# Taking batch elements one at a time through two decode layers, with transposed keys kept and softmax for two heads at once

## Chip, cores and metric

The kernel runs on one core of one Trainium2 chip. The metric is device time in microseconds (us) of one execution; lower is better.

Engine names in the profile: PE is TensorE (matmul), PEld its weight loads, DVE VectorE, ACT ScalarE, POOL GpSimd, SP the engine that issues the transfers. The kernel keeps its tiles in two on-chip memories: SBUF, into which it loads data, and PSUM, into which it has TensorE write.

## The reference, cut to what matters

Two layers of grouped-query attention and a feed-forward network (FFN), for four batch elements of one new token each. Both layers use the same weights and the same key and value cache.

```python
# B = 4, D = 512, 32 query heads, 8 key/value heads, Sk = 4096, Dh = 128, F = 1792, bf16
q = (x @ wq) ...                                     # 4 query heads share one key head
scores = einsum("bhqd,bhkd->bhqk", q, k) * Dh**-0.5
o = einsum("bhqk,bhkd->bhqd", softmax(scores), v)
attn = o @ wo
x = x + attn(layernorm(x));  x = x + ffn(layernorm(x))     # layer 1
x = x + attn(layernorm(x));  x = x + ffn(layernorm(x))     # layer 2, same caches
```

Keys of one head are 1 MB, values as much: 32 element-head pairs of each, 67 MB, plus 13.9 MB of weights. A kernel that reads the caches anew in each layer moves 148 MB.

## The kernel before

It works layer by layer. In a layer, all 32 pairs of element and head go through a key stage (transpose the keys on TensorE, copy them out of PSUM, multiply with the queries, find the maximum), then all 32 through a value stage. The scheduler orders instructions, so the stages overlap somewhat.

```python
for j in range(NPAIR):                                # key stage, one head of one element
    K_j = issue_k(j)                                  # 1 MB, 8 KB per partition
    for g in range(NG):                               # 4 x 8 transposes
        for t in range(TB):
            nc.tensor.transpose(tp[:, t, :], K_j[:, g * TB + t, :], ident_bf[:, :])
        evac_copy(KT_j[:, g * TB:(g + 1) * TB, :], tp[:, :, :])     # DVE, DVE, ACT, DVE
    for c in range(C):
        nc.tensor.matmul(sc[:, c, :], lhsT=KT_j[:, c, :], rhs=qcols, start=True, stop=True)
    nc.scalar.activation(out=SCORES[:, j, :, :], in_=sc[:, :, :], func=ACT.Copy)
    nc.vector.tensor_reduce(out=colmax[:, :], in_=sc..., op=ALU.max)    # 3 buffers
    nc.gpsimd.partition_all_reduce(gmax[:, :], colmax[:, :], P, RED.max)
    nc.gpsimd.tensor_scalar(out=NEGB[:, j, :], in0=gmax[:, :], scalar1=-scale, ...)

for j in range(NPAIR):                                # value stage
    V_j = ...                                         # 1 MB
    for h in range(rep):                              # 4 small exponentials
        nc.scalar.activation(out=pexp[:, :, h], in_=SCORES[:, j, :, h], func=ACT.Exp,
                             bias=NEGB[:, j, h:h + 1], scale=scale, accum_out=SUMS[:, j, h:h + 1])
    nc.gpsimd.partition_all_reduce(den[:, :], SUMS[:, j, :], P, RED.add)
    nc.vector.reciprocal(out=rden[:, :], in_=den[:, :])
    for c in range(C):
        nc.tensor.matmul(ot[:, :], lhsT=V_j[:, c, :], rhs=pexp[:, c, :], ...)
    nc.vector.tensor_tensor(out=OT_bf[:, b, qsl], in0=ot[:, :], in1=rden[:, :], op=ALU.mult)
    # [cut: projection, FFN, next queries after every second element]
```

## Time and profile before

| | before |
|---|---|
| median of the first three runs | 599.63 us (596.45 to 600.38) |
| transfers | 149.22 MB, 250 GB/s on the mean |
| transpositions on TensorE | 2,048 |

These are lines of the page of the profile of before: busy time by engine, two rows of the 40 slices (the granted TensorE clock in tenths, and the busy share of the transfer engines in tenths), and the transfer queue of the data.

```profile
PE 321.7 (54%) x7448; PEld 310.1 (52%) x7448; DVE 189.1 (32%) x548; ACT 170.0 (28%) x644; POOL 66.2 (11%) x198
PEclk9976965886575555555556696777657765555555
DMA  8996992855957562565997493655433978545770
q1 hardware_dynamic: 26480, 148.13, 65.5%
```

No engine is near full, and GpSimd is the least busy. The next fence is the timeline of GpSimd in a key stage; the columns are start, duration, instructions, and in brackets the idle time before them and what ended it ("issue" means that nothing the profile shows was waited for).

```profile
386.40 1.10 POOL L263 PARTITION_ALL_REDUCE gmax<-colmax  x3 [8.56 <-issue]
394.94 0.86 POOL L264 TENSOR_SCALAR NEGB<-gmax 128x4 f32<-128x4 f32 x3 [7.45 <-DVE KT_j L218]
403.60 1.10 POOL L263 PARTITION_ALL_REDUCE gmax<-colmax  x3 [7.80 <-issue]
```

Three all-reduces, a gap, three tensor_scalars, a gap: 17.2 us (403.60 - 386.40) for three heads, 2 us of it busy. Within a row of three of one kind there is no gap. The second gap is put down to a VectorE copy, but is as long as the others.

TensorE, in the same stretch, stands for 7 us in each period:

```profile
404.37 1.84 PE L256 MATMUL sc<-qT_bf,KT_j 128*128 128x4 bf16 x64 [6.87 <-DVE colmax L260]
413.59 1.05 PE L251 MATMUL tp<-ident_bf,K_j 128*128 128x128 bf16 x16 [0.22 <-ACT KT_j L220]
421.59 1.84 PE L256 MATMUL sc<-qT_bf,KT_j 128*128 128x4 bf16 x64 [6.95 <-DVE colmax L260]
```

The table of waits sums such gaps (total us, times, longest us):

```profile
POOL gmax L263 <- issue: 135.6, 16, 11.4
DVE colmax L260 <- POOL gmax L263: 117.2, 19, 10.1
POOL NEGB L264 <- issue: 116.5, 14, 12.6
POOL NEGB L264 <- DVE KT_j L218: 66.9, 9, 10.0
POOL den L281 <- issue: 58.0, 7, 11.5
```

### The profile page before, as it was taken

The numbers are of one execution on the slowest core, as the hardware profiler recorded it, in microseconds if no ns is written. First come the engines' busy times: TensorE is split into PE (matmuls) and PEld (weight loads), VectorE is DVE, ScalarE is ACT, GpSimd is POOL, SyncE is SP. The second block draws the span as 40 slices with busy tenths as digits, with TensorE's granted clock in tenths as the row PEclk, the third lists the DMA queues.
The fourth block names the chain that finished last, engine by engine and source line by source line (L and its number), as shares of the span: only waits on it lengthen the run. The fifth ranks groups of instructions, "written<-read, shape, count | busy, mean of one in ns | idle before, by whom it ended". The sixth has DMA issues, their size and how long they took to land. (4 is left out here: it accounts for less than half of the span.)

```text
span 596.7 us, 17105 instructions
## 1 busy us (share of the span) xinstructions
PE 321.7 (54%) x7448; PEld 310.1 (52%) x7448; DVE 189.1 (32%) x548; ACT 170.0 (28%) x644; POOL 66.2 (11%) x198
## 2 busy tenths in 40 slices
PE   0998833757533410267578984466655573101555
PEld 0988733656533410267568984456655473101554
DVE  2554622534322100034135672344433331000213
ACT  0243511322112420233601344122211463112710
POOL 0001111101010111020200012101110111200300
PEclk9976965886575555555556696777657765555555
DMA  8996992855957562565997493655433978545770
GB/s 334 415 373 228 354 366 88 314 213 181 390 225 282 220 242 104 212 254 206 390 420 289 161 348 133 212 212 209 157 137 142 357 295 347 215 194 212 276 292 2
DMA packets 26555, 149.22 MB, mean 250 GB/s; under 512 B 2152, under 2 KB 8048, under 8 KB 10096
## 3 DMA queue, kind: packets, MB, share of 16 engines
q1 hardware_dynamic: 26480, 148.13, 65.5%
q8 instruction: 58, 0.95, 0.6%
q14 instruction: 17, 0.14, 0.1%
HBM read 148.12 MB, written 0.00 MB: 248 GB/s over the span
## 5 line engine op out<-in xcount | busy, mean ns | idle before, releaser
L251 PE MATMUL tp<-ident_bf,K_j 128*128 128x128 bf16 x2048 | 170.8, 254 | 7.6 <-ACT KT_j L220 6.0
L251 PEld LDWEIGHTS <-K_j 128*128 128x128 bf16 x2048 | 155.6, 117 | 12.7 <-issue 11.0
L218 DVE COPY KT_j<-tp 128x1024 bf16<-128x1024 bf16 x192 | 129.6, 689 | 66.0 <-PE tp L251 55.8
L256 PE MATMUL sc<-qT_bf,KT_j 128*128 128x4 bf16 x2048 | 63.6, 166 | 124.0 <-DVE colmax L260 123.2
L256 PEld LDWEIGHTS <-KT_j 128*128 128x128 bf16 x2048 | 63.2, 104 | 126.4 <-issue 125.2
L286 PE MATMUL ot<-pexp,V_j 128*128 128x4 bf16 x2048 | 61.2, 166 | 107.2 <-DVE OT_bf L288 92.0
L286 PEld LDWEIGHTS <-V_j 128*128 128x128 bf16 x2048 | 59.0, 104 | 109.0 <-issue 92.5
L277 ACT ACTIVATE pexp<-SCORES,NEGB 128x32 bf16<-128x32 f32 x256 | 86.3, 355 | 102.9 <-PE ot L286 101.6
L220 ACT ACTIVATE KT_j<-tp 128x1024 bf16<-128x1024 bf16 x64 | 65.4, 1021 | 110.2 <-PE tp L251 108.0
L258 ACT ACTIVATE SCORES<-sc 128x128 f32<-128x128 f32 x64 | 17.8, 279 | 180.6 <-PE sc L256 180.6
L260 DVE TENSOR_REDUCE colmax<-sc 128x4 f32<-128x128 f32 x64 | 18.5, 289 | 125.1 <-POOL gmax L263 117.2
L283 DVE RECIPROCAL rden<-den 128x4 f32<-128x4 f32 x64 | 11.2, 177 | 127.9 <-POOL den L281 126.9
L277 ACT ACTIVATION_READ_ACCUMULATOR pexp<-SCORES,NEGB 128x1 f32 x256 | 48.1, 188 | 0.0
L263 POOL PARTITION_ALL_REDUCE gmax<-colmax x64 | 23.9, 428 | 199.2 <-issue 135.6
L281 POOL PARTITION_ALL_REDUCE den<-SUMS x64 | 28.1, 469 | 103.3 <-issue 58.0
L264 POOL TENSOR_SCALAR NEGB<-gmax 128x4 f32<-128x4 f32 x64 | 15.0, 234 | 194.3 <-issue 116.5
L288 DVE TENSOR_TENSOR OT_bf<-ot,rden 128x4 bf16<-128x4 f32 x64 | 9.8, 156 | 43.4 <-PE ot L286 43.0
L172 PEld LDWEIGHTS <-wo_sb 128*128 128x128 bf16 x384 | 13.0, 103 | 7.5 <-issue 7.4
L172 PE MATMUL yT<-OT_bf,wo_sb 128*128 128x2 bf16 (+1 forms) x384 | 12.9, 166 | 6.4 <-DVE OT_bf L288 6.4
L162 PEld LDWEIGHTS <-wq_sb 128*128 128x128 bf16 x384 | 11.1, 103 | 7.9 <-issue 7.9
L162 PE MATMUL qps<-xnT_bf,wq_sb 128*128 128x2 bf16 (+1 forms) x384 | 11.1, 165 | 7.5 <-DVE xnT_bf L151 7.4
L183 PE MATMUL hg<-xnT_bf,wg_sb 128*128 128x2 bf16 (+1 forms) x168 | 4.9, 165 | 7.0 <-DVE xnT_bf L151 7.0
(82 smaller groups left out, 69.5 us busy)
## 6 DMA issues: line engine op xcount, KB each, us to landing
K_j<-in_A_k_cache_dram SPq DMA_DIRECT2D x64, 1024.0 KB, 6.3
V_j<-in_A_v_cache_dram SPq DMA_DIRECT2D x64, 1024.0 KB, 9.1
wq_sb<-in_A_wq_dram SPq DMA_DIRECT2D x2, 2048.0 KB, 13.2
wo_sb<-in_A_wo_dram SPq DMA_DIRECT2D x1, 4096.0 KB, 17.9
wg_sb<-in_B_w_gate_dram SPq DMA_DIRECT2D x1, 1792.0 KB, 10.8
wu_sb<-in_B_w_up_dram SPq DMA_DIRECT2D x1, 1792.0 KB, 14.9
wd_sb<-in_B_w_down_dram SPq DMA_DIRECT2D x1, 1792.0 KB, 19.4
x_bf<-in_A_x_dram SPq DMA_DIRECT2D x1, 4.0 KB
```

Source lines behind the costliest of these rows:

```text
L162: nc.tensor.matmul(qps[:, h, :], lhsT=wq_sb[:, k, m * Dh:(m + 1) * Dh], rhs=xnT_bf[:, k, bs], start=(k == 0), stop=(k == KD - 1))
L172: nc.tensor.matmul(yT[:, dk, :], lhsT=wo_sb[:, i, dk * P:(dk + 1) * P], rhs=OT_bf[:, bs, i], start=(i == 0), stop=(i == Hq - 1))
L218: nc.vector.tensor_copy(out=out_ap, in_=in_ap)
L220: nc.scalar.activation(out=out_ap, in_=in_ap, func=ACT.Copy)
L251: nc.tensor.transpose(tp[:, t, :], K_j[:, c, :], ident_bf[:, :])
L256: nc.tensor.matmul(sc[:, c, :], lhsT=KT_j[:, c, :], rhs=qcols, start=True, stop=True)
L258: nc.scalar.activation(out=SCORES[:, j, :, :], in_=sc[:, :, :], func=ACT.Copy)
L260: nc.vector.tensor_reduce(out=colmax[:, :], in_=sc.rearrange("p c h -> p h c"), axis=AX.X, op=ALU.max)
L263: nc.gpsimd.partition_all_reduce(gmax[:, :], colmax[:, :], P, RED.max)
L277: nc.scalar.activation(out=pexp[:, :, h], in_=SCORES[:, j, :, h], func=ACT.Exp, bias=NEGB[:, j, h:h + 1], scale=scale, accum_out=SUMS[:, j ...
L281: nc.gpsimd.partition_all_reduce(den[:, :], SUMS[:, j, :], P, RED.add)
L286: nc.tensor.matmul(ot[:, :], lhsT=V_j[:, c, :], rhs=pexp[:, c, :], start=(c == 0), stop=(c == C - 1))
```

## The change

Its intent is to read and transpose the keys once instead of twice. An element's transposed keys for its eight heads stay in SBUF, so the element must finish layer 1 and compute its layer-2 scores before the next element's keys replace them. Around that, softmax is rebuilt for pairs of heads: the maximum is subtracted on VectorE, so `NEGB` on GpSimd is gone. Tiles of K and V are halved to 0.5 MB, in seven buffers; the layer-2 values of an element are multiplied while the next element is between its layers. The diff is shortened.

```diff
-            nc.gpsimd.partition_all_reduce(gmax[:, :], colmax[:, :], P, RED.max)
-            nc.gpsimd.tensor_scalar(out=NEGB[:, j, :], in0=gmax[:, :], scalar1=-scale, ...)
-            for h in range(rep):
-                nc.scalar.activation(out=pexp[:, :, h], in_=SCORES[:, j, :, h], func=ACT.Exp,
-                                     bias=NEGB[:, j, h:h + 1], scale=scale, accum_out=SUMS[...])
+    def softmax(sc, pool):                             # for GH = 2 heads
+        nc.vector.tensor_reduce(out=colmax[:], in_=sc..., op=ALU.max)
+        nc.gpsimd.partition_all_reduce(gmax, colmax, P, RED.max)
+        nc.vector.tensor_tensor(out=sh[:], in0=sc[:], in1=gmax... , op=ALU.subtract)
+        nc.scalar.activation(out=pe[:], in_=sh[:], func=ACT.Exp, scale=scale)
+        nc.vector.tensor_reduce(out=ssum[:], in_=pe..., op=ALU.add)
+        nc.gpsimd.partition_all_reduce(den, ssum, P, RED.add)
+        nc.vector.reciprocal(out=rden[:], in_=den[:])
-    attention_layer(True, after_batch_l1)
-    attention_layer(False, after_batch_l2)
+    for b in range(B):
+        for g in range(NGRP):                          # 4 pairs of heads
+            for s in range(GH): keys(b, g * GH + s)    # load, transpose, keep in KT
+            prob1[g] = softmax(scores(b, g, q1_bf), p1p)
+            if g > 0: values(b, ...) of pair g - 1
+        values(b, ...) of the last pair
+        out_proj_add(b, 1, OT_bf); ffn(b, 1); layer_norm(b, 1); q_proj(b, 1, q2_bf, 2)
+        if prob2_prev is not None: values(b - 1, ...) of all heads, layer 2
+        prob2_prev = [softmax(scores(b, g, q2_bf), p2p) for g in range(NGRP)]
     # [cut: layer norm with fewer instructions, layouts, loads of the weights]
```

## The prediction

> **What bounds the kernel now.** Not bandwidth, not TensorE. The page gives TensorE 54%, VectorE 32%, ScalarE 28%, GpSimd 11% of 596.7 us; DMA moved 149 MB at 250 GB/s, while its best 15 us stretches reached 416 to 421 GB/s.
>
> GpSimd's timeline explains the rest. In the key stage (380 to 450 us) it repeats: three `gmax` all-reduces (1.10 us together), 7.5 us idle, three `NEGB` tensor_scalars (0.86 us), 7.8 to 8.4 us idle. One period of 17.2 us serves three heads. TensorE works about 9 us of it, then stands 7 us until `colmax`, which waits for `gmax`, has freed the score buffer. So GpSimd, "11% busy", sets the pace. The Trainium skill's "GPSIMD Engine Reference", section 2.1, says that the first call to a freshly loaded kernel pays about 6 us of code load with no visible instruction. This trace agrees in kind but shows 7 to 8.5 us, at each change between all-reduce and tensor_scalar. The table of waits sums the unexplained "issue" idle before `gmax`, `NEGB` and `den` to 310 us, plus 67 us before `NEGB` put down to a VectorE copy long ended. The instruction order has 49 such changes: 49 x 7.8 = 380 us.
>
> **What the change does.**
> - GpSimd: `NEGB` is gone and two heads share a reduce: 64 all-reduces (about 0.45 us each), one code load. This is the main gain: the 17.2 us period falls away.
> - Keys are loaded and transposed once: traffic 149 to about 115 MB; 1,024 transposes (about 65 us of TensorE) and 128 PSUM copies (65 us VectorE, 33 us ScalarE) go, mostly hidden.
> - 256 exponentials with accumulator reads (86 + 48 us) become 32, estimate 0.5 us each; VectorE gains 32 subtractions and 32 sums, estimate 0.3 to 0.45 us each.
> - Added: projections, FFN and norms run four times for one element instead of twice for two: 29 ns a matmul whatever the width, about 25 us of TensorE, and two more serial chains.
> - Packets halve from 8 to 4 KB; 4 KB ones take 159 ns here, 8 KB ones 309: little loss.
>
> **New bound: DMA, then the serial chain.** Loads: 24,576 packets of 159 to 176 ns over 16 engines, 244 to 270 us, plus about 40 us of weights: 285 to 310 us if never starved. TensorE needs about 250 us, more at a low clock, nearly a tie. Between layers DMA starves: out-projection, FFN, two norms, query projection and four softmaxes make a chain of 26 to 30 us (from the last chain before: norm 4.1, FFN 6, 29 ns a projection matmul), and seven half-megabyte buffers cover about 20 us of it. I count 7 us lost in each of four, 15 us from the last V to the end (17 before), 4 at the start, 10 to 20 for evacuation waits and low clock.
>
> 295 + 28 + 19 + 10 = **352 us**, range **322 to 400** (8 in 10). Faster by over 2%: 0.97; within: 0.02; slower: 0.01.
>
> **What would show it.** No "issue" gaps of 7 to 8 us on GpSimd, no wait of `colmax` on `gmax` over about 1 us; DMA share above 80% in first-layer stages, dips to half between layers; a chain of waits of DMA and the per-element chain. If my GpSimd reading is wrong, gaps remain without tensor_scalars.
>
> **What would make it wrong.** A low clock makes transposes (128 columns) near 107 ns, so TensorE overtakes DMA; or the in-order DMA queue blocks on a buffer whose reader waits in the chain: 380 us and more. If chains hide, 320 us.

## The result

The changed kernel takes 378.66 us (median of four runs, 375.91 to 379.92), against 598.95 us. The ratio is 0.6314, with a 95% interval of 0.6282 to 0.6346. Ratios here are the mean time of one kernel's fast runs over that of the other's fast runs of the same rounds, so not quite the ratio of the medians.

The same lines of the page after the change:

```profile
PE 275.4 (73%) x7268; PEld 263.8 (70%) x7268; DVE 137.5 (36%) x476; ACT 67.7 (18%) x90; POOL 25.0 (7%) x70
PEclk9999685555558667555596685555778855555555
DMA  7998999999258999947899999758999998579920
q1 hardware_dynamic: 35696, 114.58, 83.0%
```

Transfers are busy for 83.0% of the span, 313 us (0.83 x 377.3), and dip between the elements (the 2 and 5, the 4, and the two later 5s inside the DMA row). On GpSimd the gaps have gone. Its timeline in the first-layer stage of the third element shows one all-reduce at a time, waiting for VectorE:

```profile
211.25 0.36 POOL L236 PARTITION_ALL_REDUCE gmax<-colmax  x1 [9.88 <-DVE colmax L233]
213.20 0.40 POOL L248 PARTITION_ALL_REDUCE den<-ssum  x1 [1.59 <-DVE ssum L245]
222.48 0.37 POOL L236 PARTITION_ALL_REDUCE gmax<-colmax  x1 [8.88 <-DVE colmax L233]
```

The table of waits now shows these (the last two are those of the transfer queue, for a free buffer):

```profile
DVE sh L239 <- POOL gmax L236: 10.8, 23, 0.6
PE yT L159 <- DVE OT_bf L264: 16.4, 34, 1.2
SPq L104 <- PE ot L262: 100.6, 74, 5.7
SPq L104 <- PE tp L218: 97.8, 59, 11.1
```

VectorE's longest wait for `gmax` is 0.6 us, where before it was 10.1. The table of windows shows the two kinds of stage. A line gives start and end of a stretch and its length, then the busy time and number of instructions of PE, PEld, DVE, ACT and POOL, then the granted clock (1.00 is full speed), the share of the transfer engines, and GB/s.

```profile
100.00:110.00 10.00, 10.00 (x252) 10.00 (x250) 6.24 (x16) 3.07 (x5) 2.45 (x7) 0.50 0.31 82
160.00:170.00 10.00, 7.41 (x259) 7.27 (x257) 3.01 (x19) 0.00 (x0) 0.00 (x0) 0.50 0.44 125
170.00:180.00 10.00, 7.91 (x285) 7.68 (x283) 4.37 (x14) 1.25 (x3) 2.06 (x6) 0.50 0.65 210
200.00:210.00 10.00, 9.50 (x196) 9.35 (x196) 3.42 (x7) 4.19 (x5) 0.40 (x1) 0.66 1.01 388
```

The first three lie between layers and move 82 to 210 GB/s; the last lies in the first-layer stage and moves 388.

### The profile page after: what moved, and what is told of

The parts are those of the page before. It is cut to its first block, busy times and chain, and to the rows that moved or that the text cites. A ratio compares the mean times of both kernels' runs of the same rounds, so it can differ in the third digit from the quotient of the medians.

```text
span 377.3 us, 15723 instructions
## 1 busy us (share of the span) xinstructions
PE 275.4 (73%) x7268; PEld 263.8 (70%) x7268; DVE 137.5 (36%) x476; ACT 67.7 (18%) x90; POOL 25.0 (7%) x70
## 4 chain that ended last, share of the span: by engine, by line
PE 53%; DMA 16%; DVE 15%; issue 9%; ACT 3%; POOL 3%; SPq 1%; POOLq 0%; ACTq 0%; DVEq 0%
PE tp L218 19%; PE sc L227 14%; DMA v_t<-in_A_v_cache_dram 9%; PE ot L262 7%; DMA wd_sb<-in_B_w_down_dram 6%; PE qps L148 4%; DVE kt L207 2%; PE yT L159 2%; PE hg L170 2%; DVE colmax L233 2%; DMA k_t<-in_A_k_cache_dram 2%; DVE ssum L245 2%; ACT kt L205 2%; ACT pe L243 1%; PE st L114 1%
## 5 line engine op out<-in xcount | busy, mean ns | idle before, releaser
L218 PE MATMUL tp<-ident_bf,k_t 128*128 128x128 bf16 x1024 | 97.2, 271 | 1.2 <-DMA k_t<-in_A_k_cache_dram 0.6
L218 PEld LDWEIGHTS <-k_t 128*128 128x128 bf16 x1024 | 85.2, 125 | 2.0 <-issue 1.0
L262 PE MATMUL ot<-pe,v_t 128*128 128x4 bf16 x2048 | 69.0, 166 | 17.0 <-DMA v_t<-in_A_v_cache_dram 9.7
L262 PEld LDWEIGHTS <-v_t 128*128 128x128 bf16 x2048 | 63.0, 102 | 19.1 <-DMA v_t<-in_A_v_cache_dram 11.0
L227 PE MATMUL sc<-q_bf,kt 128*128 128x4 bf16 x2048 | 69.3, 166 | 9.1 <-DVE kt L207 3.1
L227 PEld LDWEIGHTS <-kt 128*128 128x128 bf16 x2048 | 64.4, 102 | 12.8 <-DVE kt L207 5.3
L205 ACT COPY kt<-tp 128x1024 bf16<-128x1024 bf16 x52 | 52.6, 1012 | 111.0 <-PE tp L218 93.9
L207 DVE COPY kt<-tp 128x1024 bf16<-128x1024 bf16 x76 | 51.7, 687 | 53.2 <-PE tp L218 51.6
L159 PE MATMUL yT<-OT_bf,wo_sb 128*128 128x1 bf16 (+1 forms) x640 | 22.2, 165 | 25.5 <-DVE OT_bf L264 16.4
L148 PE MATMUL qps<-xn_bf,wq_sb 128*128 128x1 bf16 (+1 forms) x640 | 18.4, 165 | 8.2 <-DVE xn_bf L136 6.6
```

What stands on the lines that cost most here:

```text
L148: nc.tensor.matmul(qps[:, i, :], lhsT=wq_sb[:, k, m * Dh:(m + 1) * Dh], rhs=xn_bf[:, bs, k], start=(k == 0), stop=(k == KD - 1))
L159: nc.tensor.matmul(yT[:, :, dk], lhsT=wo_sb[:, i, dk * P:(dk + 1) * P], rhs=o_bf[:, bs, i], start=(i == 0 and dk == 0), stop=(i == Hq - 1 ...
L205: nc.scalar.copy(out=out_ap, in_=in_ap)
L207: nc.vector.tensor_copy(out=out_ap, in_=in_ap)
L218: nc.tensor.transpose(tp[:, i, :], kn[:, g * TB + i, :], ident_bf[:, :])
L227: nc.tensor.matmul(sc[:, s, c, :], lhsT=KT[kvh][:, c, :], rhs=q_bf[:, b, kvh * rep:(kvh + 1) * rep], start=True, stop=True)
```

## The experiments

Twelve runs were made, each beside the kernel before on the same chip; one of them is the changed kernel once more. "Code load" stands for the unexplained gap at a change between the two kinds of GpSimd instruction: the name is taken from the prediction, and no trace shows a load itself. Theory A: before the change, GpSimd's code loads set the pace, and after it transfers and TensorE nearly tie, with transfers starving between the layers. Rival B: what counted was the second load and transposition of the keys. Rival C: the many small exponentials. Rival D: after the change TensorE alone is the limit.

### Code loads alone, taken out of the kernel before

```diff
-            nc.gpsimd.tensor_scalar(out=NEGB[:, j, :], in0=gmax[:, :], scalar1=-scale,
+            nc.vector.tensor_scalar(out=NEGB[:, j, :], in0=gmax[:, :], scalar1=-scale,
```

> The kernel before with one word changed: NEGB is computed on VectorE, so GpSimd runs nothing but all-reduces and loads code once instead of 49 times. Traffic (149 MB), 2,048 transposes and the 256 small exponentials all stay. Theory A (code loads set the pace before): 400 to 480 us, because the 17.2 us period of three heads in the key stage falls to TensorE's own 9 to 13 us. Rival B (the second load and transposition of the keys, that is bytes and TensorE work, is what the change saved): 570 us or more, since none of it is taken away. Rival C (the 256 exponentials on ScalarE): also 570 or more.

Measured: 421.51 us against 601.24, ratio 0.7016 (0.6985 to 0.7047). Of the whole gain (1 - 0.6314 = 0.3686) one word is worth 0.2984, that is 81%. It moves as many bytes and transposes as much as before, so B and C are not what made the kernel before slow; what they save once the gaps are gone, less what the rest of the change costs, is the other 19%. The page of this run:

```profile
PE 306.0 (73%) x7448; PEld 288.5 (69%) x7448; DVE 191.8 (46%) x612; ACT 175.4 (42%) x644; POOL 51.8 (12%) x134
PEclk9977999899995555555556669999999955555555
DMA  7999999999999999987998449999999999999900
q1 hardware_dynamic: 26480, 148.13, 89.8%
L251 PE MATMUL tp<-ident_bf,K_j 128*128 128x128 bf16 x2048 | 146.6, 231 | 1.5 <-DMA K_j<-in_A_k_cache_dram 1.0
```

The DMA row is nearly full from start to end: with the gaps on GpSimd gone, transfers bound this version. Its GpSimd timeline has a head every 3.1 us:

```profile
67.33 0.37 POOL L263 PARTITION_ALL_REDUCE gmax<-colmax  x1 [2.71 <-DVE colmax L260]
70.41 0.37 POOL L263 PARTITION_ALL_REDUCE gmax<-colmax  x1 [2.71 <-DVE colmax L260]
```

Before it was 17.2 us for three, 5.7 us a head.

### Code loads put back into the changed kernel

```diff
+        gm2 = grp.tile([P, GH, rep], FP32, name="gm2", tag="gm2", bufs=2)
+        nc.gpsimd.tensor_scalar(out=gm2[:], in0=gmax[:], scalar1=1.0, scalar2=None, op0=ALU.mult)
         sh = shp.tile([P, GH, C, rep], FP32, name="sh", tag="sh")
-                                in1=gmax[:].unsqueeze(2).broadcast_to([P, GH, C, rep]),
+                                in1=gm2[:].unsqueeze(2).broadcast_to([P, GH, C, rep]),
```

> The changed kernel with one GpSimd tensor_scalar (times 1.0, same values) put between each all-reduce maximum and its subtraction: 32 tiny operations, 44 more code loads in the instruction order. Theory A: about 7.8 us for most of those loads, 44 x 7.8 = 340 us of GpSimd time, largely on the path: 550 us or more, GpSimd gaps of 7 to 8 us back. Rival B: 32 operations of 0.25 us, under 390 us.

Measured: 496.27 us (one run, so its state is unknown), 118 us slower than 378.66. 32 operations of under 0.3 us each did that, so rival B is out here as well; but the time is under the 550 that was expected. The waits of GpSimd in this run:

```profile
POOL gm L239 <- issue: 185.6, 22, 12.5
POOL den L250 <- issue: 73.3, 12, 7.0
POOL gmax L236 <- issue: 16.5, 2, 10.1
```

The gaps are there, 275 us in these three lines, 8.4 us in the mean before `gm` (185.6 / 22), the result of the added operation. Only 118 us reached the end of the span. The size of a gap was right; "largely on the path" was not: other work went on during more than half of it. The kernel before is alike: its gaps sum to 377 us (the four GpSimd lines shown above), and taking them away gained 180. What the gaps are worth depends on what stands beside them: taken out of the kernel before, they are 81% of the gain; put back into the changed kernel, a smaller sum of them (275 us against 377) is 53% (118 of 220 us).

### Keys loaded and transposed again

```diff
-        prob2_prev = [softmax(scores(b, g, q2_bf), p2p) for g in range(NGRP)]
+        prob2_prev = []
+        for g in range(NGRP):
+            for s in range(GH):
+                keys(b, g * GH + s)
+            prob2_prev.append(softmax(scores(b, g, q2_bf), p2p))
```

> The changed kernel, but each element's keys are loaded and transposed again ahead of its second attention, as in the kernel before (traffic back to 149 MB, 2,048 transposes), with GpSimd as in the changed kernel. Tells what keeping the keys is worth once the code loads are gone. Theory A with a DMA bound: 34 MB more at 370 GB/s is 91 us, so 450 to 480 us, if the reload can't fill the DMA gaps between the layers; 420 to 440 if it fills them. Rival B: 550 or more.

Measured: 455.26 us, ratio 0.7591 (0.7549 to 0.7632). Keeping the keys is worth 77 us in this structure (0.7591 - 0.6314, times 600), against 91 us for the bytes at the mean rate. So it is not hidden. But this run moves the same bytes as the kernel before with `NEGB` on VectorE, has GpSimd as free, and is 34 us slower than it (455.26 against 421.51). That is what all the rest of the change costs on balance: going element by element, with smaller tiles, more and narrower projections, and softmax in pairs. No run separates these. It leaves the change 43 us ahead of the one-word edit.

Where do the 34 us go? The transfer queue of this run:

```profile
q1 hardware_dynamic: 44912, 148.14, 88.0%
```

By this share, packets take 399 us here (88.0% of 453.3) and 377 us there (89.8% of 420.4): 22 us are slower transfers, 12 us more idle ones.

### One head at a time

```diff
-GH = 2
+GH = 1
```

> The changed kernel with GH = 1: softmax for one head at a time, 128 all-reduces instead of 64, and the small VectorE operations doubled. Theory A: with no code loads, GpSimd and VectorE have room in the first-layer stage; only the four chains of second-layer softmaxes get longer (8 instead of 4 small rounds): 0 to 4% slower, 378 to 394 us. If pairing heads matters by itself: over 400 us.

Measured: 408.23 us, ratio 0.6798 (0.6754 to 0.6841): 30 us slower than with pairs. My expectation failed. GpSimd has room, but TensorE waits in order behind VectorE. In the groups of instructions of this run (columns: busy us and mean ns of one, then idle time before the group with what ended it):

```profile
L218 PE MATMUL tp<-ident_bf,k_t 128*128 128x128 bf16 x1024 | 114.6, 304 | 0.4 <-DVE kt L207 0.2
L159 PE MATMUL yT<-OT_bf,wo_sb 128*128 128x1 bf16 x512 | 17.2, 165 | 35.0 <-DVE OT_bf L264 30.0 <-DMA wo_sb<-in_A_wo_dram 5.0
```

and in the changed kernel:

```profile
L218 PE MATMUL tp<-ident_bf,k_t 128*128 128x128 bf16 x1024 | 97.2, 271 | 1.2 <-DMA k_t<-in_A_k_cache_dram 0.6 <-DVE kt L207 0.2 <-ACT kt L205 0.2
L159 PE MATMUL yT<-OT_bf,wo_sb 128*128 128x1 bf16 x512 | 17.6, 165 | 23.5 <-DVE OT_bf L264 14.4 <-DMA wo_sb<-in_A_wo_dram 9.1
```

A head's normalising multiplication (`OT_bf`) sits in VectorE's queue behind the next head's chain of maximum, subtraction, exponential and sum, with GpSimd and ScalarE in it; the out-projection behind it stops TensorE. That wait doubles, from 14.4 to 30.0 us. It is not more frequent (32 waits in all against 34), but 18 of the waits last over 1 us, against 8 in the changed kernel. The same count of transpositions also takes 17 us longer, which the colder clock accounts for: by the shares of the next section, 34% of 1,024 transpositions take 51 ns more each, an estimate of 18 us. These two are what "two heads at once" saves; GpSimd is busy for 13% of this run, so its own time is not short. How much each adds to the 30 us was not tested, nor why the clock is colder.

### What the transpositions cost

No kernel was needed for this: from each trace I took the spacing of starts of successive transpositions and the granted clock recorded at the time. Transpositions with no record near are counted with the slow ones; they have the slow spacing.

```
granted clock 1.0: 56 ns between starts (median); 0.5: 107 ns (median), in every trace
share of transpositions at 1.0: before 61% (1184 of 1951), NEGB on VectorE 87%, after 42% (401 of 958), one head at a time 8%
```

The Trainium skill's "TensorE: Matmul & The Clock Gate", Part 1, gives 55 to 56 ns warm and 106 to 107 ns cold for 128 columns; these traces agree to the nanosecond. The timeline of the changed kernel shows it as well: the same 16 transpositions within 3 us, after a run of narrow matmuls:

```profile
205.95 1.72 PE L218 MATMUL tp<-ident_bf,k_t 128*128 128x128 bf16 x16
207.50 0.74 PE L227 MATMUL sc<-q_bf,kt 128*128 128x4 bf16 x24
208.11 1.05 PE L218 MATMUL tp<-ident_bf,k_t 128*128 128x128 bf16 x16
```

### Fewer buffers, larger tiles

Run with four buffers in place of seven:

```diff
-KV_BUFS = 7
+KV_BUFS = 4
```

> The changed kernel with KV_BUFS 4 instead of 7. Theory A (DMA starves between the layers because the buffers run full while the chain runs): three half-megabyte buffers less are 1.5 MB less of loads running ahead, 3 x 1.3 us in each of four chains plus some in the attention stages: about 394 us (388 to 405). Rival D (what holds the changed kernel up is TensorE alone, loads are always early): under 382 us.

Measured: 425.13 us, ratio 0.7103 (0.7054 to 0.7152), 46 us slower: buffers matter, and more than the 16 us that I had worked out.

Run with 1 MB tiles:

```diff
-CH = 16
+CH = 32
-KV_BUFS = 7
+KV_BUFS = 3
```

> The changed kernel with K and V loaded as in the kernel before, 1 MB a head in 8 KB packets (CH = 32), in three buffers (3 MB, against 3.5 MB). If small packets cost what the traces suggest (4 KB at 369 GB/s on the mean here, 8 KB at 398 GB/s in the run of the kernel before with NEGB on VectorE): 100 MB take 253 instead of 273 us of all engines, 20 us less, of which some is lost to coarser waits and one half-megabyte buffer less: 360 to 376 us. If packet size is of no account: 385 us or more, since waits are coarser.

and, as a control with the same bytes of buffers, six half-megabyte tiles (`KV_BUFS = 6`):

> The control for the run with 1 MB tiles: the same 3 MB of buffers, but as six half-megabyte tiles in 4 KB packets. Between 378.7 us with seven and 425 us with four buffers, a straight line gives 394 us. If 4 KB packets cost time, this is slower than the 406 us of three 1 MB tiles; if coarse tiles cost more than packets give, it is 386 to 398 us.

Measured: 406.13 us with three 1 MB tiles, 382.92 us (ratio 0.6397) with six of half a megabyte. I had expected the larger packets to gain 20 us; at equal bytes coarse tiles lose 23 us instead. The transfer queues of the two runs, 1 MB tiles first, tell why:

```profile
q1 hardware_dynamic: 21872, 114.57, 76.5%
q1 hardware_dynamic: 35696, 114.58, 82.2%
```

That is 309 us of transfers (of a span of 404.3) against 314 (of 381.5): 8 KB packets saved about 4 us and not 20, while the coarse tiles left the queue idle for 95 us instead of 68. So the prediction's "little loss" from 4 KB packets was right, and the finer tiles are a gain of the change. The loss by buffers isn't a straight line: one less costs 4 us, three less 46. Why it bends so was not tested.

### Values moved into the chain between the layers

```diff
+    def mm(*args, **kw):                     # in place of nc.tensor.matmul
+        ins = nc.tensor.matmul(*args, **kw)
+        if pinned[0]:
+            tc.keep_in_program_order(ins)    # stays behind what was issued before it
+        return ins
     # [cut] in ffn: fill(0, 1) after the norm, fill(2, 3) after hu; in the loop:
-        out_proj_add(b, 1, OT_bf); ffn(b, 1); layer_norm(b, 1); q_proj(b, 1, q2_bf, 2)
-        [values(b - 1, ...) of all heads]
-        prob2_prev = [softmax(scores(b, g, q2_bf), p2p) for g in range(NGRP)]
+        out_proj_add(b, 1, OT_bf); pinned[0] = b > 0
+        ffn(b, 1, fill); layer_norm(b, 1); fill(4, 5); q_proj(b, 1, q2_bf, 2)
+        prob2 = [softmax(scores(b, 0, q2_bf), p2p)]; fill(6)
+        prob2.append(softmax(scores(b, 1, q2_bf), p2p)); fill(7); pinned[0] = False
+        prob2 += [softmax(scores(b, g, q2_bf), p2p) for g in range(2, NGRP)]
```

> The changed kernel with TensorE's order fixed between the layers (for the second to fourth element): the previous element's 256 value matmuls are all put into the chain, in the waits for layer norm and GELU and up to the second group of scores, instead of 112 of them behind the last score. Buffers come free earlier, so loads go on. Theory A: of some 9 us of idle DMA in each of three such chains about 5 are won back: 358 to 370 us. Rival D: no gain, 376 us or more, as the value matmuls only lengthen the chain.

Measured: 377.27 us, ratio 0.6291 (0.6248 to 0.6335): no difference from the changed kernel (0.6314, and 0.6274 later). The expectation failed. Its profiled run was slow (379.8 us), so its trace is not used to explain a difference, and there is none to explain. What it rules out is that emptying buffers earlier inside the chain is enough by itself. No gain is also what rival D had been given here, so this run does not speak against D; the fewer buffers above and the next run do. As to order alone, its trace lacks about 10 us of transfers between 150 and 210 us, as that of the changed kernel does, only some 10 us later, and the stretch from the first gate matmul to the end of the query projection is 17 to 18 us long (13 to 15 in the changed kernel).

### Half of V in the first layer

Results are wrong: half of each V tile of layer 1 is loaded and used twice. (The comparison still passed, so its tolerance is wide enough not to see this.) The scheduler also placed a few matmuls elsewhere.

```diff
+        if half:                             # layer 1 only
+            dq.dma_start(out=tl[:, :CH // 2], in_=src[:, :CH // 2])
-                nc.tensor.matmul(ot[:], lhsT=v[:, i, :], rhs=pe[:, s, c, :],
+                nc.tensor.matmul(ot[:], lhsT=v[:, i % (CH // 2) if half else i, :], rhs=pe[:, s, c, :],
```

> Wrong results on purpose: in the first attention only half of each tile of V is loaded (2 KB packets) and its chunks are used twice, so TensorE's work is the same and 16.8 MB less are moved, all in the first-layer stage. If that stage waits for DMA alone: 16.8 MB at 370 GB/s, 45 us less, 333 us. If TensorE and DMA nearly tie there, as predicted: 345 to 366 us. If TensorE alone holds the stage up: 372 or more.

Measured: 363.52 us (one run, so its state is unknown), 15 us less for 16.8 MB. The transfer queue:

```profile
q1 hardware_dynamic: 35696, 97.80, 77.1%
```

Packets take 279 us (of a span of 361.7), 34 us less than in the changed kernel and not 45: in the packet records 2 KB take 96 ns in the mean and 4 KB 185, against 177 for 4 KB in the changed kernel. So 15 of 34 us reached the end, under half of what a stage bound by transfers alone would give. TensorE takes over soon: the two nearly tie, and D is wrong as well, for TensorE alone would have given nothing.

### Pairs in the values too: a version that is a little faster

The two heads of a pair share one value tile in PSUM and one multiplication, and a pair's out-projection comes one pair later.

```diff
-    def values(b, kvh, prob, o_bf):
-        ot = ps_ot.tile([P, rep], FP32, name="ot", tag="ot")
+    def values(b, g, prob, o_bf):
+        ot = ps_ot.tile([P, GH, rep], FP32, name="ot", tag="ot")
+        for s in range(GH):                   # [cut: load and multiply into ot[:, s]]
+        nc.vector.tensor_tensor(out=<heads of pair g>, in0=ot[:], in1=rden[:], op=ALU.mult)
+    def out_proj_part(b, g, yT):              # the matmuls of pair g, the first one pinned
     # in the loop over pairs
+            if g > 0: values(b, g - 1, prob1[g - 1], OT_bf)
+            if g > 1 and b > 0: out_proj_part(b, g - 2, yT1)
```

> A try for a better version: the two heads of a pair share one value tile in PSUM and one normalising multiplication, and a pair's out-projection is issued one pair later (from the second element on), so TensorE no longer stands still for VectorE behind the softmax of the next pair. In the changed kernel TensorE idles 14 us before out-projection and 11 us before value and gate matmuls for that multiplication. If TensorE and DMA share the limit in the first-layer stage, as the half-V run says: 360 to 371 us. If DMA alone sets the pace: 376 us or more.

Measured: 371.30 us, ratio 0.6196 (0.6171 to 0.6220). To be sure that this is not a difference of chips, both ran once more:

> The changed kernel itself, unaltered, on the same chip and in the same rounds as the next run: 375 to 381 us, ratio to the kernel before 0.628 to 0.635.

> The pairwise version once more beside the changed kernel: if its 2% are real, 369 to 374 us and a ratio below that of the changed kernel in the same rounds, the intervals apart; if they were a difference of chips, no difference.

Measured: the changed kernel 376.51 us, ratio 0.6274 (0.6236 to 0.6312); the pairwise version 371.90 us, ratio 0.6211 (0.6176 to 0.6245). In the same rounds it is ahead by 1.0% (0.6211 / 0.6274), and the intervals just overlap. It is the fastest that I ran, by a small margin. The waits of its first run:

```profile
PE ot L262 <- DVE OT_bf L265: 4.9, 6, 1.3
PE ot L262 <- DMA v_t<-in_A_v_cache_dram: 29.3, 28, 9.4
```

and in the changed kernel:

```profile
PE ot L262 <- DMA v_t<-in_A_v_cache_dram: 9.7, 13, 2.2
```

The out-projection's wait for VectorE, 16.4 us in the changed kernel, is down to 1.0 (with 2.4 us of idle time at other out-projections that nothing explains), and values now wait 29 us for their transfer, where it was 9.7. (On the same chip, in the second call, it was 29.5 against 13.0.) TensorE gave up its wait, and took most of it back from the transfers: what a near tie looks like.

## Why the prediction was right, and where it was off

The prediction was 352 us (322 to 400); measured were 378.66.

- **"GpSimd, 11% busy, sets the pace": right, shown.** The one-word edit gained 180 us; the reverse edit cost 118. The prediction's sum of gaps, 49 x 7.8 = 380 us, is about what the table of waits has (377 us in 46 gaps), but it is not what they cost. A single gap varies more than its "7 to 8.5 us": over the whole trace, from 5.9 to 12.6.
- **"This is the main gain": right.** 81% of it by the same edit, 53% by the reverse one. Beyond the one-word edit, keeping the keys (77 us) minus the cost of the rest of the change (34 us) made up the other 43.
- **"Keys ... mostly hidden": half right.** The prediction counted the bytes in its new bound, as they should be: putting the keys back cost 77 us. That the TensorE part of it was hidden is not shown; TensorE nearly ties.
- **Pairing heads: not seen.** The prediction gave it no time beyond the all-reduces. It is worth 30 us, and with one head at a time TensorE waits longer for VectorE and transposes at a lower clock.
- **Transfers 295 us: too low by 18.** They took 313. The 4 KB packets were 177 ns in the mean, just above the range used (159 to 176), and the median was 159: a few slow packets make the mean.
- **Starving between layers, 28 us: too low by 12.** Summing the missing share of the 10 us windows gives 13 us after the first element, 10, 8.5 and 8.5 after the others: 40. The prediction has seven buffers cover about 20 us of the chain; their 3.7 MB are 10 us at 370 GB/s, the mean while transfers run, an estimate that fits a larger loss but was not tested.
- **Tail 15 and start 4 us: right.** The windows miss 16 and 2 us there.
- **"10 to 20 us for evacuation waits and low clock": too high as a sum, and the low clock acted elsewhere.** 313 + 40 + 16 + 2 is 371 of 377, so 6 us are left for it. But TensorE's own work was under-counted: 1,024 transpositions, about 65 us in the prediction, took 97 us, and 58% of them ran at half clock. This made TensorE 275 us busy instead of 250, and a limit in the first-layer stage.

The errors did not cancel: two terms were 18 and 12 us too low and one some 4 us too high, which is the way from 352 to the span of 377. The wide range covered it.

What stays open: why three buffers less cost 46 us; where most of the 22 us of slower transfers come from, since the runs with 1 MB tiles put packet size at about 4 us; how the 34 us divide among the parts of the change, and how much of them comes from the colder TensorE, for no run changed the clock alone; and what happens in a GpSimd gap. The small exponentials (C) had no run of their own.

## What to carry to other kernels

Read the least busy engine's timeline before you call it idle: GpSimd at 11% set the pace by switching between two kinds of instructions, and moving one 0.2 us operation to VectorE was worth 180 us. Price each part of a large rewrite by undoing it alone: here most of the gain had nothing to do with the rewrite's stated aim, and the rest of the restructuring cost 34 of the 77 us that the kept keys saved. Undo it from both ends, for the shares differ. When two engines nearly tie, a wait that you take from one comes back on the other, so expect a fraction of it.

## What the Trainium skill lacked or had wrong

- "GPSIMD Engine Reference", section 2.1, speaks of about 6 us at the first call to a freshly loaded kernel. The runs show 5.9 to 12.6 us, 8.2 in the mean (377 us in 46 gaps; 8.4 us in the mean before the tensor_scalar put back in), and at each change between an all-reduce and a plain tensor_scalar, in both directions, all through the kernel. That alternating the two pays each time is not said there.
- "TensorE: Matmul & The Clock Gate", Part 1, has the clock rise after some 3.4 us of sustained activity; its spacings for 128 columns (56 and 107 ns) agree with these traces. It doesn't say that narrow matmuls may not count: from 100 to 110 us of the changed kernel TensorE is busy 10.00 of 10 us, most of its 252 matmuls 4 columns wide, and the granted clock is 0.50. That the width is the reason is not shown: the stretch has transpositions too, and no run changed the width alone.
